# Head 4's second row tile in the opening, and K's block transposes by feature quarters

One core of a Trainium2 chip. The metric is the device time of one execution, in microseconds (us); smaller is better.

## The reference

Sliding-window attention over a cache, between two projections. Eight batches of 32 rows, 32 query heads on 4 K/V heads, a window of the last 2048 keys, 128 features a head, all bf16.

```python
W = min(4096, max(256, Sk // 4))                       # 2048
q = (x @ wq).reshape(B, Sq, Hq, Dh).transpose(0, 2, 1, 3)
k = jnp.repeat(k_cache[:, :, Sk - W:, :], rep, axis=1)
v = jnp.repeat(v_cache[:, :, Sk - W:, :], rep, axis=1)
p = softmax(einsum("bhqd,bhkd->bhqk", q, k) * Dh ** -0.5)
o = einsum("bhqk,bhkd->bhqd", p, v)
return o.transpose(0, 2, 1, 3).reshape(B, Sq, Hq * Dh) @ wo
```

## The kernel before

The 32 pairs of batch and K/V head are "units". A unit has four chunks; a chunk is one step ("slot") of TensorE's program: four matmuls of scores into a PSUM tile `s_ps` (PSUM is the memory that this program's matmuls write to), Exp on ScalarE, and two slots later the product with V. Other work (projections, K's transposes) is put into the slots by a plan. The engines run their instructions in program order.

K must lie with its features on the partitions. Units 0 to 2 get that by TensorE transposes, most others by DMA transposes (`kT`), and the eleven units of `V_T` by VectorE and GpSimd (`kTv`): VectorE turns 32x32 blocks (`blocks`), then 16 moves of 32x512 bring each block row to its partitions (`move`). The numbers of a unit in `V_T`: after which unit's load its raw K is loaded, the slots of the four block transposes, the slots between which the moves lie, and how many moves GpSimd makes.

```python
V_T = {4: (None, (4, 6, 6, 7), 8, 13, 8),
       7: (4, (18, 18, 19, 20), 20, 27, 12), ...
       **{u: (u - 4, range(4*u - 14, 4*u - 10), 4*u - 11, 4*u - 2, 12) for u in (12, 14, ...)}}
...
        def blocks(i):                      # a quarter of the 16 key columns j
            sl = slice(i * KT // 4, (i + 1) * KT // 4)
            nc.vector.transpose(out=st["kb"][:, sl, :], in_=self.k_raw[ui][:, sl, :])
        def move(k, d):                     # needs all four
            out = self.kT[ui][d * 32:(d + 1) * 32, :, k * 32:(k + 1) * 32]
            in_ = st["kb"][k * 32:(k + 1) * 32, :, d * 32:(d + 1) * 32]
            i, n = 4 * k + d, 16 - V_T[ui][4]
            if i * n // 16 != (i + 1) * n // 16:
                nc.vector.tensor_copy(out=out, in_=in_)
            else:
                nc.gpsimd.tensor_scalar(out=out, in0=in_, ...)
...
        # the opening, after x has been transposed
        for c in range(self.DC):            # 8 chunks of wq: all heads, first row tile (heads 0-3: both)
            for h in range(self.rep):
                q_mm(c, h)
        tp = [self.ps_s.tile([P, KT, P], BF16, name="kf_ps", tag="s_ps") for _ in range(2)]
        k_turn(0)                           # eight transposes of K of unit 0
        q_copy(...); q_copy(...); q_copy(...); q_copy(...)
        k_copy(0)                           # VectorE: PSUM to kT, 128x1024
        self.late = self.q_late(4, 2)
        self.late[0]()                      # head 4, second row tile: eight matmuls
        k_turn(1)
        k_copy(1)
...
        # then the slots; slot 0: scores, head 5's second row tile; slot 1: scores, head 6's
```

The pool `ps_s`, of which the score tiles come, has two buffers, and the tiles `tp` of the opening come out of it too.

Of the kernel before, what the change touches and what calls it, by code (L numbers as in the profile page):

```python
# [21 lines left out]

PE_T = (0, 1, 2)

V_T = {4: (None, (4, 6, 6, 7), 8, 13, 8),
       7: (4, (18, 18, 19, 20), 20, 27, 12),
       9: (5, (23, 24, 25, 26), 26, 34, 10),
       **{u: (u - 4, range(4 * u - 14, 4 * u - 10), 4 * u - 11, 4 * u - 2, 12) for u in (12, 14, 17, 19, 22, 24, 27, 29)}}
# [80 lines left out]
class Fast:  # L109
# [72 lines left out]
    def load_k(self, ui, part=None):  # L182
# [3 lines left out]
        src = self.k_cache[b, g, self.Sk - self.W:, :]  # L186
        if ui not in V_T and ui not in self.kT:
            self.kT[ui] = self.ktp.tile([P, KT, P], BF16, name="kT")
        if ui in PE_T or ui in V_T:
            H = KT // 2  # L190
# [58 lines left out]
    def kv_pieces(self, ui):  # L249


        nc, P, KT = self.nc, self.P, self.KT
        st = {}

        def blocks(i):
            if i == 0:
                st["kb"] = self.kbp.tile([P, KT, P], BF16, name="kb")
            sl = slice(i * KT // 4, (i + 1) * KT // 4)
            nc.vector.transpose(out=st["kb"][:, sl, :], in_=self.k_raw[ui][:, sl, :])  # L259

        def move(k, d):
            if k == d == 0:
                self.kT[ui] = self.kvt.tile([P, KT, P], BF16, name="kTv", tag="kv")
            out = self.kT[ui][d * 32:(d + 1) * 32, :, k * 32:(k + 1) * 32]
            in_ = st["kb"][k * 32:(k + 1) * 32, :, d * 32:(d + 1) * 32]
            i, n = 4 * k + d, 16 - V_T[ui][4]
            if i * n // 16 != (i + 1) * n // 16:
                nc.vector.tensor_copy(out=out, in_=in_)  # L268
            else:
                nc.gpsimd.tensor_scalar(out=out, in0=in_, scalar1=1.0, scalar2=1.0, op0=ALU.mult, op1=ALU.mult)  # L270
        return [lambda i=i: blocks(i) for i in range(4)], [lambda k=k, d=d: move(k, d) for k in range(4) for d in range(4)]

    def q_view(self, g):
        return self.QT[g][:, :].rearrange("p (b h s) -> p b h s", b=self.B, h=self.rep)
# [15 lines left out]
        n = 2 if g == 3 else 4  # L290
        return [lambda h=h, i=i: piece(h, i) for h0 in range(0, self.rep, n) for i in range(2) for h in range(h0, h0 + n)]

    def q_late(self, h0, n):
        nc, P, DC, B = self.nc, self.P, self.DC, self.B
        st = {}

        def piece(i):
            if i == 0:
                st["ps"] = self.ps_m.tile([P, n, P], FP32, name="ql_ps", tag="m")
            for c in range(DC):  # L300
                nc.tensor.matmul(st["ps"][:, i, :], lhsT=self.wq_t[0, c // (DC // 2)][:, c % (DC // 2), (h0 + i) * P:(h0 + i + 1) * P],  # L301
                                 rhs=self.xT[:, c, P:self.NQ], start=(c == 0 and i == 0), stop=(c == DC - 1), skip_group_check=True)
            if i == n - 1:
                copy = nc.scalar.copy if h0 == self.rep - 1 else nc.vector.tensor_copy
                copy(out=self.q_view(0)[:, B // 2:, h0:h0 + n, :].rearrange("p b h s -> p h b s"),
                     in_=st["ps"][:, :, :].rearrange("p h (b s) -> p h b s", b=B // 2))
        return [lambda i=i: piece(i) for i in range(n)]

    def o_pieces(self, g, t, cuts=(512, 512), st=None):

# [28 lines left out]
    def start(self):  # L339
        nc, P = self.nc, self.P  # L340
        warm = self.ps_s.tile([P, 512], FP32, name="warm_ps", tag="s_ps")
        one = nc.const_aps.tensor
        x_sb = self.vp.tile([P, self.NT, self.D], BF16, name="x_sb", tag="v")
        xf = self.x.rearrange("b s d -> (b s) d")
        H = self.DC // 2

        nc.sync.dma_start(out=x_sb[:, 0, :], in_=xf[0:P, :])
        nc.scalar.dma_start(out=x_sb[:, 1, :], in_=xf[P:2 * P, :])
        wq0 = self.load_wq(0, 0, (1, 1, 1, 1)) + self.load_wq(0, 1, (2, 1, 1))
        for p in wq0:  # L350
            p()
        self.load_k(0, 0)
        self.load_k(0, 1)
        self.load_v(0, nc.sync)
        self.load_k(1)
        self.weights = []
        for g in range(self.Hkv):
            if g + 1 < self.Hkv:
                self.weights += self.load_wq(g + 1, 0) + self.load_wq(g + 1, 1)
            if g:  # L360
                self.weights += self.load_wo(2 * g - 2) + self.load_wo(2 * g - 1)
        self.weights += self.load_wo(2 * self.Hkv - 2) + self.load_wo(2 * self.Hkv - 1)
        self.load_v(1, nc.sync)
        self.load_k(2)
        self.load_k(4)
        self.load_v(2, nc.sync)
        self.load_unit(3)
        for v in self.va:
            nc.gpsimd.memset(v[:, :, self.Dh:self.VW], 1.0)
        nc.gpsimd.memset(self.ones_c[:, :], 1.0)  # L370
        def warm_up(n):
            for i in range(n):
                nc.tensor.matmul(warm[:, :], lhsT=one(1.0, [P, P], BF16), rhs=one(1.0, [P, 512], BF16), start=True, stop=True)
        warm_up(N_WARM)


        def x_turn(half, pl, tag):
            ps = pl.tile([P, H, self.NT, P], BF16, name="xT_ps", tag=tag)
            for c in range(H):
                for t in range(self.NT):  # L380
                    nc.tensor.transpose(ps[:, c, t, :], x_sb[:, t, half * H + c:self.D:self.DC], self.ident[:, :])  # L381
            for i, copy in ((0, nc.vector.tensor_copy), (1, nc.scalar.copy)):
                c0 = half * H + i * H // 2
                copy(out=self.xT[:, c0:c0 + H // 2, :], in_=ps[:, i * H // 2:(i + 1) * H // 2, :, :].rearrange("p c t s -> p c (t s)"))

        x_turn(0, self.ps_m, "m")
        x_turn(1, self.ps_s, "s_ps")
        qs = [self.ps_o.tile([P, 2, self.NQ], FP32, name="q0_ps", tag="o_ps") for _ in range(2)]
        qs.append(self.ps_m.tile([P, 4, P], FP32, name="q0_ps", tag="m"))
        KT = self.KT  # L390
        tp = None

        def k_turn(half):
            for j in range(half * KT // 2, (half + 1) * KT // 2):
                nc.tensor.transpose(tp[half][:, j % (KT // 2), :], self.k_raw[0][:, j, :], self.ident[:, :])  # L395

        def k_copy(half):
            sl = slice(half * KT // 2, (half + 1) * KT // 2)
            nc.vector.tensor_copy(out=self.kT[0][:, sl, :], in_=tp[half][:, 0:KT // 2, :])

        def q_mm(c, h):
            ps, n = (qs[h // 2][:, h % 2, :], self.NQ) if h < 4 else (qs[2][:, h - 4, :], P)
            nc.tensor.matmul(ps, lhsT=self.wq_t[0, c // H][:, c % H, h * P:(h + 1) * P],  # L403
                             rhs=self.xT[:, c, 0:n], start=(c == 0 and h in (0, 2, 4)), stop=(c == self.DC - 1),
                             skip_group_check=True)

        def q_copy(copy, h0, h1, b0, b1):
            ps = qs[h0 // 2] if h0 < 4 else qs[2]
            copy(out=self.q_view(0)[:, b0:b1, h0:h1, :].rearrange("p b h s -> p h b s"),
                 in_=ps[:, :, b0 * self.Sq:b1 * self.Sq].rearrange("p h (b s) -> p h b s", s=self.Sq))  # L410

        for c in range(self.DC):
            for h in range(self.rep):
                q_mm(c, h)
            if c == 0:
                warm_sb = self.c1.tile([P, 8], BF16, name="warm_sb")
                nc.vector.tensor_copy(out=warm_sb[:, :], in_=warm[:, 0:8])
        tp = [self.ps_s.tile([P, KT, P], BF16, name="kf_ps", tag="s_ps") for _ in range(2)]
        k_turn(0)
        q_copy(nc.scalar.copy, 0, 2, 0, 1)  # L420
        q_copy(nc.vector.tensor_copy, 2, 4, 0, 1)
        q_copy(nc.scalar.copy, 4, 8, 0, 1)
        q_copy(nc.scalar.copy, 4, 8, 1, self.B // 2)
        k_copy(0)
        self.late = self.q_late(4, 2)
        self.late[0]()
        k_turn(1)
        k_copy(1)
        self.va_copy(0)
        q_copy(nc.vector.tensor_copy, 0, 2, 1, self.B)  # L430
        self.q0_rest = lambda: q_copy(nc.vector.tensor_copy, 2, 4, 1, self.B)
# [22 lines left out]
    def side_plan(self):  # L454
# [4 lines left out]
        def spread(pieces, s0, s1):  # L459
            for k, p in enumerate(pieces):  # L460
                plan[s0 + (s1 - s0) * k // len(pieces)].append(p)
# [4 lines left out]
        for g, w in Q_SLOTS.items():  # L466
            pieces = self.q_pieces(g)
            n = 0 if g == 3 else 4
            spread(pieces[:n], *w[0])
            spread(pieces[n:], *w[1])  # L470
        for g, w in O_SLOTS.items():
            spread(self.o_pieces(g, 0) + (self.o_pieces(g, 1) if g < self.Hkv - 1 else []), *w)
        for ui, (_, s0, s1, s2, _) in V_T.items():
            blocks, moves = self.kv_pieces(ui)
            for k, p in enumerate(blocks):
                plan[s0[k]].append(p)
            spread(moves, s1, s2)
        return plan

    def run(self):  # L480
# [214 lines left out]
```

## Time and profile before

| | before |
|---|---|
| median of the first three executions | 183.78 us (183.70 to 184.23) |
| span of the profiled execution | 182.3 us |
| TensorE / VectorE / ScalarE / GpSimd busy | 97% / 69% / 75% / 49% |
| GpSimd's wait for VectorE's block transposes | 32.1 us in 8 places |

TensorE is the bound. The other engines' idle time is of no account unless TensorE waits for them.

### The profile page before, as it was taken

Reading aid. Unit: us, or ns where it says so; the run is one execution under the profiler, and the core shown is the slowest. Engines: PE = TensorE matmul, PEld = TensorE weight load, DVE = VectorE, ACT = ScalarE, POOL = GpSimd, SP = SyncE. Lnnn points to the kernel's source line nnn. Section 1 sums busy time; section 2 is a strip of 40 time slices with the busy share of each in tenths; the row PEclk is TensorE's granted clock in tenths of the full one; section 3 lists DMA queues with packets and bytes.
Section 4 is the critical chain, followed back from the end, with each engine's and each line's share of the span. In section 5 each row is a group of like instructions: output and inputs, shape, how many; then the busy total and the mean of one; then the engine's idle time right before and its main releaser. Section 6 shows DMA issues by size and latency. Waiting matters only on the chain.

```text
span 182.3 us, 5017 instructions
## 1 busy us (share of the span) xinstructions
PE 177.4 (97%) x2026; PEld 152.0 (83%) x2041; DVE 126.0 (69%) x257; ACT 136.2 (75%) x147; POOL 89.2 (49%) x138
## 2 busy tenths in 40 slices
PE   7999999999999999999999999999999999999993
PEld 2899998998999999988787899988787788888853
DVE  0237799769887698487799565967587987554253
ACT  2228898896897888997878787887878788888800
POOL 2003564088770895936939707929606949600000
PEclk9999999999999999999999999999999999999999
DMA  6999999999999999999999999999999999980013
GB/s 169 395 400 408 225 388 350 233 296 260 377 391 244 322 257 365 374 295 313 304 378 377 391 269 271 369 245 365 258 318 273 331 289 344 218 167 0 0 41 85
DMA packets 52954, 51.73 MB, mean 284 GB/s; under 512 B 39744, under 2 KB 40256, under 8 KB 52928
## 3 DMA queue, kind: packets, MB, share of 16 engines
q1 hardware_dynamic: 52352, 50.90, 99.3%
q10 hardware_dynamic: 576, 0.49, 0.8%
q8 instruction: 16, 0.26, 0.6%
q14 instruction: 10, 0.08, 0.1%
HBM read 41.42 MB, written 0.52 MB: 230 GB/s over the span
## 4 chain that ended last, share of the span: by engine, by line
PE 91%; DMA 6%; SPq 1%; issue 1%; DVE 0%
PE o_ps L516 30%; PE s_ps L505 30%; PE op_ps L322 14%; PE q_ps L285 10%; DMA kT<-in_k_cache_dram 4%; PE q_ps L403 3%; DMA x_sb<-in_x_dram 2%; PE ql_ps L301 1%; PE tp L244 1%; SPq L208 1%; PE xT_ps L381 1%; PE kf_ps L395 0%; SPq L200 0%; DVE o_t L332 0%; PE cnt_ps L571 0%
## 5 line engine op out<-in xcount | busy, mean ns | idle before, releaser
L507 ACT ACTIVATE pT<-s_ps 128x1024 bf16<-128x1024 f32 x128 | 128.3, 1027 | 27.7 <-PE s_ps L505 27.4
L270 POOL TENSOR_SCALAR kTv<-kb 32x512 bf16<-32x512 bf16 x126 | 84.3, 669 | 51.3 <-DVE kb L259 32.1
L516 PE MATMUL o_ps<-va,pT 128*128 128x129 bf16 x1024 | 78.8, 220 | 0.1
L516 PEld LDWEIGHTS <-pT 128*128 128x128 bf16 x1024 | 68.5, 98 | 3.1
L505 PE MATMUL s_ps<-QT,kT 128*128 128x256 bf16 x336 | 50.4, 273 | 0.2
L505 PEld LDWEIGHTS <-kT 128*128 128x128 bf16 x336 | 31.7, 98 | 9.8 <-DMA kT<-in_k_cache_dram 0.4
L322 PE MATMUL op_ps<-wo_sb,OT 128*128 128x512 bf16 (+2 forms) x129 | 32.8, 353 | 0.6
L259 DVE STREAM_TRANSPOSE kb<-k_raw 128x512 bf16<-128x512 bf16 x44 | 29.7, 691 | 1.6 <-DMA k_raw<-in_k_cache_dram 1.2
L285 PE MATMUL q_ps<-xT,wq_sb 128*128 128x256 bf16 x192 | 28.3, 273 | 0.0
L438 DVE COPY va<-v_sb 128x2048 bf16<-128x2048 bf16 x30 | 25.4, 847 | 2.0 <-DMA v_sb<-in_v_cache_dram 1.6
L505 PE MATMUL s_ps<-QT,kTv 128*128 128x256 bf16 x176 | 26.4, 273 | 0.2
L268 DVE COPY kTv<-kb 32x512 bf16<-32x512 bf16 x50 | 23.1, 462 | 1.2
L444 DVE RECIPROCAL RL_all<-o_ps 128x2 f32<-128x2 f32 x32 | 5.3, 165 | 26.3 <-PE o_ps L516 26.1
L505 PEld LDWEIGHTS <-kTv 128*128 128x128 bf16 x176 | 16.9, 98 | 6.5 <-issue 0.4
L285 PEld LDWEIGHTS <-wq_sb 128*128 128x128 bf16 x192 | 16.9, 98 | 1.2
L450 DVE STREAM_TRANSPOSE OT<-o_sb 128x256 bf16<-128x256 bf16 x32 | 14.3, 445 | 1.1
L448 DVE TENSOR_TENSOR o_sb<-o_ps,RL_all 128x256 bf16<-128x256 f32 x32 | 13.6, 424 | 1.1
L322 PEld LDWEIGHTS <-OT 128*128 128x128 bf16 x144 | 11.4, 98 | 2.3 <-DVE OT L450 0.2
L436 POOL TENSOR_SCALAR va<-v_sb 128x2048 bf16<-128x2048 bf16 x2 | 3.8, 1897 | 17.0 <-DMA v_sb<-in_v_cache_dram 17.0
L288 ACT CAST QT<-q_ps 128x512 bf16<-128x512 f32 x12 | 7.0, 583 | 0.2 <-PE q_ps L285 0.2
L329 DVE TENSOR_TENSOR oacc<-op_ps,oacc 128x512 f32<-128x512 f32 x8 | 5.3, 662 | 2.0 <-PE op_ps L322 2.0
L332 DVE TENSOR_TENSOR o_t<-op_ps,oacc 128x512 bf16<-128x512 f32 (+2 forms) x6 | 3.1, 514 | 3.8 <-remote 2.2
(35 smaller groups left out, 45.0 us busy)
## 6 DMA issues: line engine op xcount, KB each, us to landing
v_sb<-in_v_cache_dram SPq DMA_DIRECT2D x30, 512.0 KB, 6.6
wo_sb<-in_wo_dram SPq DMA_DIRECT2D x16, 512.0 KB, 6.4
wq_sb<-in_wq_dram SPq DMA_DIRECT2D x13, 512.0 KB, 6.6
k_raw<-in_k_cache_dram SPq DMA_DIRECT2D x13, 512.0 KB, 5.7
wq_sb<-in_wq_dram SPq DMA_DIRECT2D x6, 256.0 KB, 4.5
v_sb<-in_v_cache_dram SPq DMA_DIRECT2D x4, 256.0 KB, 5.2
kT<-in_k_cache_dram SPq DMA_TRANSPOSE x36, 7.1
k_raw<-in_k_cache_dram SPq DMA_DIRECT2D x2, 256.0 KB, 5.7
```

The costliest lines, as they stand in the source:

```text
L259: nc.vector.transpose(out=st["kb"][:, sl, :], in_=self.k_raw[ui][:, sl, :])
L268: nc.vector.tensor_copy(out=out, in_=in_)
L270: nc.gpsimd.tensor_scalar(out=out, in0=in_, scalar1=1.0, scalar2=1.0, op0=ALU.mult, op1=ALU.mult)
L285: nc.tensor.matmul(st[k][:, hl % 2, :], lhsT=self.wq_t[g, i][:, c % (DC // 2), hl * P:(hl + 1) * P], rhs=self.xT[:, c, :], start=(c == 0 a ...
L288: nc.scalar.copy(out=self.q_view(g)[:, :, 2 * k:2 * k + 2, :].rearrange("p b h s -> p h b s"), in_=st[k][:, :, :].rearrange("p h (b s) -> ...
L322: nc.tensor.matmul(ps[:, 0:w], lhsT=self.OT[:, gq, c, t * P:(t + 1) * P], rhs=self.wo_t[gq][:, c, n0:n0 + w], start=(k == 0), stop=(k == 7))
L438: self.nc.vector.tensor_copy(out=out, in_=in_)
L448: nc.vector.tensor_tensor(out=o_sb[:, :, :, :], in0=o_ps[:, :, 0:Dh].rearrange("p q (i c) -> p q c i", c=4), in1=rl[:, ui * QT_N:(ui + 1) ...
L450: nc.vector.transpose(out=self.OT[:, g * QT_N:(g + 1) * QT_N, :, b * self.Sq:(b + 1) * self.Sq], in_=o_sb[:, :, :, :])
L505: nc.tensor.matmul(s_ps[:, jj, :], lhsT=self.kT[ui][:, c * CJ + jj, :], rhs=q_u, start=True, stop=True)
L507: nc.scalar.activation(out=pT[:, :, :], in_=s_ps[:, :, :], func=ACT.Exp, bias=0.0, scale=self.scale)
L516: nc.tensor.matmul(o_ps[:, qt, 0:self.VW], lhsT=pT[:, jj, qt * P:(qt + 1) * P], rhs=va[:, j, 0:self.VW], start=(j == 0 and qt == 0), stop= ...
```

## The change

x has 256 rows, two row tiles of 128. The intent of the change: (1) to do head 4's second row tile in the projection loop, where TensorE waits for wq, and to copy K out in quarters, so that the first scores start sooner; (2) to let GpSimd move K when one feature quarter has been turned, and not all four, and to give VectorE the moves of the last quarter alone.

```diff
-V_T = {4: (None, (4, 6, 6, 7), 8, 13, 8),
+V_T = {4: (None, (4, 6, 6, 7), 8, 13, 9),
@@ blocks and moves
-            sl = slice(i * KT // 4, (i + 1) * KT // 4)
-            nc.vector.transpose(out=st["kb"][:, sl, :], in_=self.k_raw[ui][:, sl, :])
+            sl = slice(i * P // 4, (i + 1) * P // 4)
+            nc.vector.transpose(out=st["kb"][:, :, sl], in_=self.k_raw[ui][:, :, sl])
-            i, n = 4 * k + d, 16 - V_T[ui][4]
-            if i * n // 16 != (i + 1) * n // 16:
+            if 4 * d + k >= V_T[ui][4]:
-        return ..., [... for k in range(4) for d in range(4)]
+        return ..., [... for d in range(4) for k in range(4)]
@@ opening (q_late takes the chunks to do as an argument)
+        self.late = self.q_late(4, 2)
         for c in range(self.DC):
             for h in range(self.rep):
                 q_mm(c, h)
+            self.late[0](cs=(c,))
...
-        k_copy(0)
-        self.late = self.q_late(4, 2)
-        self.late[0]()
+        k_copy(nc.vector.tensor_copy, 0, KT // 4)
+        k_copy(nc.vector.tensor_copy, KT // 4, KT // 2)
         k_turn(1)
-        k_copy(1)
+        k_copy(nc.vector.tensor_copy, KT // 2, KT)
@@ side_plan
-            spread(moves, s1, s2)
+            spread(moves[:n], s0[1] + 1, s2)
+            spread(moves[n:], s1, s2)
```

More of the change, by code (lines that the diff above doesn't have):

```diff
@@ L270, in move @@
                 nc.gpsimd.tensor_scalar(out=out, in0=in_, scalar1=1.0, scalar2=1.0, op0=ALU.mult, op1=ALU.mult)
-        return [lambda i=i: blocks(i) for i in range(4)], [lambda k=k, d=d: move(k, d) for k in range(4) for d in range(4)]
+        return [lambda i=i: blocks(i) for i in range(4)], [lambda k=k, d=d: move(k, d) for d in range(4) for k in range(4)]
     def q_view(self, g):
@@ L291, in q_pieces, with q_late, piece @@
         return [lambda h=h, i=i: piece(h, i) for h0 in range(0, self.rep, n) for i in range(2) for h in range(h0, h0 + n)]
-    def q_late(self, h0, n):
+    def q_late(self, h0, n, st=None):
         nc, P, DC, B = self.nc, self.P, self.DC, self.B
-        st = {}
-        def piece(i):
-            if i == 0:
+        st = {} if st is None else st
+        def piece(i, cs=None):
+            if "ps" not in st:
                 st["ps"] = self.ps_m.tile([P, n, P], FP32, name="ql_ps", tag="m")
-            for c in range(DC):
+            for c in range(DC) if cs is None else cs:
                 nc.tensor.matmul(st["ps"][:, i, :], lhsT=self.wq_t[0, c // (DC // 2)][:, c % (DC // 2), (h0 + i) * P:(h0 + i + 1) * P],
@@ L306, in piece @@
                      in_=st["ps"][:, :, :].rearrange("p h (b s) -> p h b s", b=B // 2))
-        return [lambda i=i: piece(i) for i in range(n)]
+        return [lambda i=i, **kw: piece(i, **kw) for i in range(n)]
     def o_pieces(self, g, t, cuts=(512, 512), st=None):
@@ L395, in k_turn, with k_copy @@
                 nc.tensor.transpose(tp[half][:, j % (KT // 2), :], self.k_raw[0][:, j, :], self.ident[:, :])
-        def k_copy(half):
-            sl = slice(half * KT // 2, (half + 1) * KT // 2)
-            nc.vector.tensor_copy(out=self.kT[0][:, sl, :], in_=tp[half][:, 0:KT // 2, :])
+        def k_copy(copy, j0, j1):
+            copy(out=self.kT[0][:, j0:j1, :], in_=tp[2 * j0 // KT][:, j0 % (KT // 2):j0 % (KT // 2) + j1 - j0, :])
         def q_mm(c, h):
@@ L472, in side_plan @@
             spread(self.o_pieces(g, 0) + (self.o_pieces(g, 1) if g < self.Hkv - 1 else []), *w)
-        for ui, (_, s0, s1, s2, _) in V_T.items():
+        for ui, (_, s0, s1, s2, n) in V_T.items():
             blocks, moves = self.kv_pieces(ui)
```

## The prediction

> **What bounds the kernel now.** I read the page first: row 1 (engines), row 2 (slices) and row 4 (the chain that ended last).
>
> ```profile
> span 182.3 us, 5017 instructions
> PE 177.4 (97%) x2026; PEld 152.0 (83%) x2041; DVE 126.0 (69%) x257; ACT 136.2 (75%) x147; POOL 89.2 (49%) x138
> DMA  6999999999999999999999999999999999980013
> PE 91%; DMA 6%; SPq 1%; issue 1%; DVE 0%
> ```
>
> TensorE is 91% of the chain and neither VectorE (69% busy) nor GpSimd (49%) is near its limit. So work that moves between VectorE and GpSimd is worth only what a TensorE wait on it costs. What can be won is TensorE's idle time, and I looked for all of it by going through the timeline from 4.4 us (first transposes of x) to the end, comparing the distance between two matmul starts with what the same pair takes elsewhere (0.056 us behind a 128-column matmul, 0.11 us behind a 256-column one). I found four places of over 0.05 us behind the opening's x transposes that the change could touch, 0.16 + 0.06 + 0.27 + 0.29 = 0.78 us in all, 0.4% of the span:
>
> ```profile
> 8.64 0.61 PEld L403 LDWEIGHTS <-wq_sb 128*128 128x128 bf16 x7 [0.16 <-DMA wq_sb<-in_wq_dram]
> ...
> 12.69 0.33 PEld L505 LDWEIGHTS <-kT 128*128 128x128 bf16 x4
> ...
> 26.94 3.25 DVE L268 COPY kTv<-kb 32x512 bf16<-32x512 bf16 x6
> ...
> 30.31 0.34 PEld L505 LDWEIGHTS <-kTv 128*128 128x128 bf16 x4 [0.36 <-issue]
> ```
>
> First line: in the opening's Q projection TensorE stands 0.16 us for the second half of wq. Second: the first scores start at 12.69, 0.06 us later than the dense row of transposes before them would allow; the copy of K out of PSUM (11.94 + 0.69 = 12.63) holds them. Third and fourth: the scores of unit 4 start when VectorE's last move of that unit's transposed K is done, 26.94 + 3.25 = 30.19; the dense row would have put the matmul at 30.07, and it started at 30.34, so 0.27 us are lost. GpSimd's moves were done at 29.75.
>
> The fourth wait decides this prediction. It comes from the chain of waits, in order of time, window 43 to 44.2 us:
>
> ```profile
> 36.74 6.67 DMA kT<-in_k_cache_dram
> 43.42 0.05 issue
> 43.46 0.61 PE s_ps L505 x4
> ```
>
> Chunk 2 of unit 6 waits for the second half of its K, which the DMA transpose lands at 43.42; TensorE would have been ready at about 43.17, 0.29 us sooner. Is that transfer late because a buffer came free late, or because the DMA engines are full? The table by stretches (columns after the five engines: TensorE clock, DMA share, GB/s):
>
> ```profile
> 2.50:10.00 7.50, 7.33 (x70) 5.26 (x69) 0.92 (x3) 1.07 (x2) 0.00 (x0) 1.00 1.02 383
> 10.00:20.00 10.00, 10.00 (x147) 9.53 (x145) 5.95 (x12) 6.87 (x10) 1.90 (x1) 1.00 1.11 354
> 20.00:30.00 10.00, 10.00 (x140) 9.47 (x137) 9.71 (x19) 9.23 (x11) 7.16 (x9) 1.00 1.05 365
> 30.00:40.00 10.00, 9.89 (x122) 9.05 (x120) 8.07 (x19) 8.32 (x11) 2.77 (x5) 1.00 1.17 261
> ```
>
> The share is over 1.0 in all of them: the 16 DMA engines are full from 2.5 us on, so the queue runs as fast as it can and the landing at 43.42 does not depend on how soon TensorE comes. Walking the program's load order, no transfer ahead of this one reuses a buffer that is freed later than it is needed: unit 6's kT takes unit 0's, v of unit 6 that of unit 0.
>
> **What the skill says.** The Trainium skill, "SBUF — State Buffer", section "Who interferes with whom": a VectorE copy in a two-port mode and a GpSimd instruction exclude each other for a whole instruction, and DMA contends with neither. The trace agrees on the first: VectorE's 32x512 moves take 0.283 us at the least and up to 0.661 beside GpSimd's (median 0.582, window 18 to 47), and one GpSimd move was drawn out from 0.61 to 0.95 us by a copy of V. "VectorE: DVE Perf Modes", section "The three transpose paths": VectorE's transpose turns 32x32 blocks only. That is why the 16 moves per unit exist, and why a transposed feature quarter is all that four of the moves need. "Perfetto Trace Analysis", section "Optimization Strategy": find the gaps on the bounding engine and what releases them; that is the method above.
>
> **The change, part by part.** *Opening, matmuls.* Eight 128-column matmuls of head 4's second row tile move from between the two K transposes into the projection loop, one per chunk. In the loop they cost 8 x 0.056 = 0.45 us. Four of them come before the wq wait, 4 x 0.056 = 0.22, and cover its 0.16. The loop so ends 0.45 - 0.16 = 0.29 us later, and the K transposes start at 11.24 + 0.29 = 11.53 in place of 11.24. But these eight were what TensorE did while VectorE copied K. After the change only the second eight transposes (0.45 us) lie there. *Opening, copies.* The copy of 128x1024 in 0.69 us becomes two of 128x512; the x copy of that shape (PSUM to SBUF, bf16) takes 0.424 each, and two of those back to back overlap by about 0.08 (13.44 + 0.68 against a next start at 14.04), so 0.34 + 0.42 = 0.77. The copy began 0.70 us after the transposes began (11.94 - 11.24); so now 12.23, first quarter done at 12.65, second at 12.99. The first score tile takes the PSUM buffer of this very tile (two buffers, taken in turn), so I expect it to wait for both: 12.99 + 0.05 = 13.04 in place of 12.69, 0.35 later. The eight matmuls are done before 12.69 in both kernels, so none of that is made up: TensorE simply stands about 0.6 us there. If only the first quarter counts, the start is 12.70 and nothing is lost or won.
>
> *Unit 4.* GpSimd gets 9 moves for 8, VectorE 7 for 8, and GpSimd's begin behind block quarter 0 (19.23 + 0.71 = 19.94) and not behind the fourth (23.21 + 0.69 = 23.90). Two of its moves come in program order before its copy of V for unit 2: 2 x 0.67 = 1.34, so that copy starts near 21.3 and not 20.60, ends near 23.3, and the first matmul that reads it is at 24.15: no wait. The other 7 moves end at 23.3 + 7 x 0.67 + 0.34 (one drawn out) = 28.3. VectorE keeps its order with one move fewer; its five behind 26.94 run beside GpSimd until 28.3 and then at 0.28: done about 28.9, over 1 us ahead of need. The 0.27 wait goes.
>
> *Units 7 to 29.* 12 or 10 moves per unit start up to 5 us sooner on GpSimd (its 32.1 us of waiting on VectorE's blocks mostly end), but TensorE had no wait for these units: nothing on the path. Block transposes of 128 x (16 runs of 32) keep 512 elements a lane; I estimate 0.67 to 0.75 us as now (0.691).
>
> *Sum.* TensorE reaches unit 6, chunk 2 at 43.17 + 0.35 - 0.27 = 43.25, or with the kinder opening at 42.9. Both are before 43.42. It waits there and starts at 43.46 as before, and everything behind it is the same dense row of matmuls. Net change: 0. A gain of 0.2 to 0.5 us in the first 30 us is given back in a wait for DMA.
>
> **The rivals.** (1) *The gains add up to the end*: 0.27, with the kinder opening perhaps 0.3 to 0.4, and the time is 183.4. For it: the DMA landing varies between executions, and where it comes sooner, gains pass. Against it: shares over 1.0 for 40 us, and unit 5's second half lands at 37.65 for a need at 37.86, so a second transfer stands close behind the first. (2) *VectorE or GpSimd becomes late somewhere*: more contention while V is copied (0.65 us alone, 1.04 beside GpSimd), or strided transposes cost much more than 0.69; at 0.1 us each, 44 of them add 4.4 us to VectorE's 126, which 56 idle us take up; a stall of a unit or two would add 0.3 to 1 us: 184.3. (3) *The opening costs more than 0.6 us net*, so that TensorE is behind the DMA at 43.4: plus 0.1 to 0.3 us. Against it: the path above is short.
>
> **Range and chances.** The three times of before lie at 183.70, 183.78 and 184.23, so half a microsecond is noise. Centre 183.7: no change from 183.78, with a small part of rival 1. Low 183.2 is rival 1 in full with some noise, high 184.3 is rival 2 or the slow one of the three. 2% is 3.7 us, nearly five times all the idle time that I found, and no new wait of that size is in sight: within 2% 0.98, 0.01 on either side.
>
> **What would show it.** In the changed trace: no wait on wq at 8.6; K transposes near 11.5; first scores near 13.0 (right) or 12.7 (buffer rule wrong); GpSimd's first move near 20 and unit 4's scores without a gap; the wait for kT of unit 6 grown to between 0.2 and 0.6 us, with its start still near 43.4; the same distances from there to the end. The prediction is wrong if that start moves with TensorE, or if a wait on kTv, va or o_ps turns up behind 44 us.

## The result

| | before | changed |
|---|---|---|
| median | 183.74 us (183.55 to 184.23, 4 runs) | 183.94 us (183.76 to 184.15, 4 runs) |
| span of the profiled execution | 182.3 us | 182.1 us |
| ratio | | 1.0007, 95% interval 0.9984 to 1.0030 |

A ratio is the mean time of one kernel's fast runs over that of the other's of the same rounds, so not quite the ratio of the medians. The changed kernel takes the same time within noise. Its page:

```profile
span 182.1 us, 5033 instructions
PE 178.0 (98%) x2041; PEld 152.1 (84%) x2041; DVE 125.3 (69%) x257; ACT 136.3 (75%) x147; POOL 89.8 (49%) x139
DMA  5999999999999999999999999999989999990003
PE 93%; DMA 3%; SPq 1%; DVE 1%; issue 0%
```

DMA fell from 6% to 3% of the chain and VectorE came in with 1%. Both have a place in the timeline. First the projection loop (timeline of the changed kernel, 4.2 to 9.4 us):

```profile
8.83 0.66 PEld L401 LDWEIGHTS <-wq_sb 128*128 128x128 bf16 x8 [0.28 <-DMA wq_sb<-in_wq_dram]
```

The wait for wq is still there. Four of the moved matmuls lie ahead of it, but wq landed at 8.79 in this execution and at 8.60 in the other. Then the first scores (timeline, 11 to 15.1 us):

```profile
11.66 0.94 PEld L394 LDWEIGHTS <-k_raw 128*128 128x128 bf16 x16
...
12.36 1.35 DVE L397 COPY kT<-kf_ps 128x512 bf16<-128x512 bf16 x3 [0.50 <-PE kf_ps L394]
...
13.17 0.33 PEld L505 LDWEIGHTS <-kT 128*128 128x128 bf16 x4 [0.57 <-DVE kT L397]
```

All sixteen transposes now come in one row and TensorE then idles 0.57 us for VectorE's copies: this is the chain's new 1%. The first scores start at 13.17 and not 12.69. The first quarter's copy ended at 12.78 (12.36 + 0.425), the second's at 13.12; the scores followed the second. Unit 4, with VectorE's moves and the loads of its scores (timeline, 26.9 to 31.7 us):

```profile
27.05 2.24 DVE L267 COPY kTv<-kb 32x512 bf16<-32x512 bf16 x5
...
30.45 0.42 PEld L505 LDWEIGHTS <-kTv 128*128 128x128 bf16 x4
```

Its K is complete at 29.29, and the scores' load no longer shows a wait. GpSimd's timeline between 19 and 30 us tells why:

```profile
20.11 1.30 POOL L269 TENSOR_SCALAR kTv<-kb 32x512 bf16<-32x512 bf16 x2 [1.43 <-DVE RL_all L443]
21.49 1.90 POOL L435 TENSOR_SCALAR va<-v_sb 128x2048 bf16<-128x2048 bf16 x1
23.48 5.07 POOL L269 TENSOR_SCALAR kTv<-kb 32x512 bf16<-32x512 bf16 x7
```

Two moves run behind the first block quarter, ahead of the copy of V; the other seven are done at 28.55, where before eight ran from 24.05 to 29.75. Unit 6, chunk 2, in the chain of waits between 43 and 44.2 us:

```profile
42.98 0.17 PE o_ps L516 x3
43.16 0.44 PE q_ps L284 x4
43.59 0.44 PE s_ps L505 x4
```

No DMA any more: these scores start at 43.43 (the chain prints 43.59, where the matmul ahead of them has ended), in their turn in the dense row. The transfer landed at 41.86.

GpSimd's waits for the block transposes, before and changed (`--waits`: us in total, times, longest), and the block transposes themselves, before and changed (page, with the mean ns of one):

```profile
POOL kTv L270 <- DVE kb L259: 32.1, 8, 7.3
POOL kTv L269 <- DVE kb L259: 27.2, 7, 7.1
L259 DVE STREAM_TRANSPOSE kb<-k_raw 128x512 bf16<-128x512 bf16 x44 | 29.7, 691 | 1.6 <-DMA k_raw<-in_k_cache_dram 1.2
L259 DVE STREAM_TRANSPOSE kb<-k_raw 128x512 bf16<-128x512 bf16 x44 | 29.5, 687 | 1.0 <-DMA k_raw<-in_k_cache_dram 0.7
```

Most of the waiting that the change went for is still there. GpSimd has as much to do as before (49% busy) and now idles mostly ahead of a unit's first quarter, not ahead of its fourth. What grew is the margin: from the last move of a unit's K to the unit's first scores it is 0.20 to 1.76 us for the units 9 to 29 of `V_T` in this trace of before, and 2.73 to 5.13 us in that of the changed kernel.

### The profile page after: what moved, and what is told of

Read it like the earlier page. It is cut to its first block, busy times and chain, and to the rows that moved or that the text cites. A ratio compares the mean times of both kernels' runs of the same rounds, so it can differ in the third digit from the quotient of the medians.

```text
span 182.1 us, 5033 instructions
## 1 busy us (share of the span) xinstructions
PE 178.0 (98%) x2041; PEld 152.1 (84%) x2041; DVE 125.3 (69%) x257; ACT 136.3 (75%) x147; POOL 89.8 (49%) x139
## 4 chain that ended last, share of the span: by engine, by line
PE 93%; DMA 3%; SPq 1%; DVE 1%; issue 0%
PE o_ps L516 32%; PE s_ps L505 31%; PE op_ps L321 15%; PE q_ps L284 12%; DMA wq_sb<-in_wq_dram 3%; PE q_ps L401 2%; PE tp L244 1%; SPq L168 1%; PE ql_ps L300 1%; DVE kT L397 0%; PE kf_ps L394 0%; SPq L346 0%; DVE o_t L331 0%; PE cnt_ps L571 0%
## 5 line engine op out<-in xcount | busy, mean ns | idle before, releaser
L507 ACT ACTIVATE pT<-s_ps 128x1024 bf16<-128x1024 f32 x128 | 128.4, 1028 | 27.2 <-PE s_ps L505 26.9
L269 POOL TENSOR_SCALAR kTv<-kb 32x512 bf16<-32x512 bf16 x127 | 84.9, 669 | 47.7 <-DVE kb L259 27.2
L321 PE MATMUL op_ps<-wo_sb,OT 128*128 128x512 bf16 (+2 forms) x144 | 36.0, 355 | 0.0
L284 PE MATMUL q_ps<-xT,wq_sb 128*128 128x256 bf16 x192 | 28.3, 273 | 0.0
L267 DVE COPY kTv<-kb 32x512 bf16<-32x512 bf16 x49 | 22.6, 462 | 1.2
L435 POOL TENSOR_SCALAR va<-v_sb 128x2048 bf16<-128x2048 bf16 x2 | 3.8, 1900 | 15.2 <-DMA v_sb<-in_v_cache_dram 15.1
L401 PE MATMUL q_ps<-xT,wq_sb 128*128 128x256 bf16 (+1 forms) x64 | 5.9, 246 | 0.1
```

The source lines that it names most:

```text
L269: nc.gpsimd.tensor_scalar(out=out, in0=in_, scalar1=1.0, scalar2=1.0, op0=ALU.mult, op1=ALU.mult)
L284: nc.tensor.matmul(st[k][:, hl % 2, :], lhsT=self.wq_t[g, i][:, c % (DC // 2), hl * P:(hl + 1) * P], rhs=self.xT[:, c, :], start=(c == 0 a ...
L321: nc.tensor.matmul(ps[:, 0:w], lhsT=self.OT[:, gq, c, t * P:(t + 1) * P], rhs=self.wo_t[gq][:, c, n0:n0 + w], start=(k == 0), stop=(k == 7))
L401: nc.tensor.matmul(ps, lhsT=self.wq_t[0, c // H][:, c % H, h * P:(h + 1) * P], rhs=self.xT[:, c, 0:n], start=(c == 0 and h in (0, 2, 4)), ...
L507: nc.scalar.activation(out=pT[:, :, :], in_=s_ps[:, :, :], func=ACT.Exp, bias=0.0, scale=self.scale)
```

## The experiments

Most effects here are a few tenths of a microsecond, and the time of one kernel scatters by half a microsecond or more between executions. So I measured distances inside the traces. "Chunk 4" is the first matmul of the projection's chunk 4, behind the wait for wq; behind it no distance depends on when wq landed. "Scores 0", "scores 4" and "scores 31" are the first matmuls of scores of these units. "Waits on kTv" are TensorE waits on VectorE's and GpSimd's moves.

| trace | chunk 4 at | to scores 0 | on to scores 4 | on to scores 31 | chunk 4 to scores 31 | waits on kTv |
|---|---|---|---|---|---|---|
| before, first | 8.64 | 4.04 | 17.65 | 137.44 | 159.14 | unit 4: 0.27 |
| before_again | 8.89 | 4.05 | 17.38 | 137.46 | 158.89 | unit 17: 0.32 |
| changed | 8.84 | 4.33 | 17.38 | 137.18 | 158.90 | none |
| e1_opening | 9.30 | 4.32 | 17.38 | 137.14 | 158.85 | none |
| e2_quarters | 8.62 | 4.11 | 17.39 | 137.20 | 158.69 | none |
| e3_onekf | 8.93 | 4.77 | 17.43 | 137.14 | 159.34 | none |
| f4_filled | 8.69 | 4.33 | 17.33 | 137.28 | 158.94 | none |
| f5_between | 9.21 | 4.11 | 17.38 | 137.14 | 158.64 | none |
| f6_onecopy | 8.87 | 4.26 | 17.38 | 137.14 | 158.78 | none |
| f7_nostart | 9.05 | 4.33 | 17.38 | 137.14 | 158.85 | none |
| g1_before_plus8 | 8.79 | 4.48 | 17.38 | 137.56 | 159.42 | unit 7: 0.41 |
| g2_after_plus8 | 8.75 | 4.77 | 17.38 | 137.39 | 159.54 | none |
| g3_best | 9.18 | 3.76 | 17.43 | 137.14 | 158.33 | none |

17.38 and 137.14 are the dense rows: many traces have just these, so anything above is a wait. The distances end at unit 31. From its scores to the end of the span it is 14.33 to 14.35 us in eight traces, 14.43 in g1 and g2, 14.50 in the first trace of before, 14.65 in e3_onekf and 14.72 in f7_nostart; what makes these five longer was not looked into. Timed runs:

| run | median, us | before, same rounds | ratio | 95% interval |
|---|---|---|---|---|
| e1_opening | 184.40 | 184.14 | 1.0033 | 0.9995 to 1.0071 |
| e2_quarters | 183.87 | 184.14 | 0.9994 | 0.9964 to 1.0023 |
| e3_onekf | 184.93 | 184.14 | 1.0064 | 1.0034 to 1.0094 |
| g1_before_plus8 | 184.74 | 184.09 | 1.0037 | 1.0012 to 1.0063 |
| g2_after_plus8 | 184.52 | 184.09 | 1.0029 | 1.0005 to 1.0053 |
| g3_best | 183.92 | 184.09 | 0.9985 | 0.9967 to 1.0003 |

The changed kernel itself was not timed again in these rounds, so it is compared with the others by its trace alone. before_again and f4 to f7 had one look each (184.62; 184.53, 184.54, 183.78, 184.40), whose state is unknown, and whose times say nothing at this size. All outputs were correct.

**The opening alone.** `V_T`, blocks, moves and plan of before in the changed kernel:

```diff
-V_T = {4: (None, (4, 6, 6, 7), 8, 13, 9),
+V_T = {4: (None, (4, 6, 6, 7), 8, 13, 8),
-            sl = slice(i * P // 4, (i + 1) * P // 4)           # and the rest of kv_pieces
+            sl = slice(i * KT // 4, (i + 1) * KT // 4)
-            spread(moves[:n], s0[1] + 1, s2)
-            spread(moves[n:], s1, s2)
+            spread(moves, s1, s2)
```

> The change's opening with the block transposes and moves of before. Theory A (the opening costs 0.35 to 0.48 us and the unit 4 part wins 0.27 only where TensorE comes early): first scores near 13.15, TensorE so late that unit 4's K (ready near 30.2) no longer holds it, unit 4's scores near 30.55 without a gap, unit 6 chunk 2 near 43.4, time that of the changed kernel, within 0.15 us. Theory B (the two parts simply add): 0.27 us slower than the changed kernel.

Unit 4's scores had no gap, and chunk 4 to scores 31 took 158.85, as in the changed kernel: theory A. The clock times of the expectation failed (13.63 for 13.15): in this execution TensorE ran x's transposes at 0.107 us each and not 0.061 (so it did in f7_nostart and g3_best) and was half a microsecond late from the start. That is why the distances count. That the times agree within 0.15 us was not tested.

**The block quarters alone.** The change's moves, and the opening of before:

```diff
-        k_copy(nc.vector.tensor_copy, 0, KT // 4)              # and the rest of the opening
-        k_copy(nc.vector.tensor_copy, KT // 4, KT // 2)
+        k_copy(0)
+        self.late = self.q_late(4, 2)
+        self.late[0]()
```

> The opening of before with the change's block transposes and moves. Theory A: first scores near 12.69, unit 4's scores at 30.07 without a gap; from there only a late K transfer (unit 5 or 6) can hold TensorE. If these transfers land as in the trace of before (43.42), unit 6 chunk 2 starts at 43.46 and the time is that of before; if as in the changed kernel's trace (41.86), it starts near 42.9 and the time is 0.3 to 0.5 us under the changed kernel's. Theory B (the unit 4 part is worth nothing or costs something): not faster than the kernel before, and a gap before unit 4's scores stays.

The second branch came: first scores at 12.72, unit 4 at 30.11 without a gap, the transfer for unit 6 landed at 41.31, its scores started at 42.94. Its size did not: from chunk 4 it is 0.21 us shorter than the changed kernel, where 0.3 to 0.5 was expected. The times (0.9994) are too coarse to confirm it.

**Before**, nothing edited.

> The kernel before, unchanged, for a second trace of it. Theory A (its wait at 43.46 is for a transfer whose landing differs between executions): first scores 12.69 and the gap before unit 4's scores again, 0.27; the K transfer of unit 6 may land anywhere between 41.8 and 43.5, so the gap at unit 6 chunk 2 between 0 and 0.3. Rival (the landing is fixed by a full queue): 43.4 again.

Half of it held. The transfer landed at 41.33 and chunk 2 of unit 6 started at 43.15 with no wait, so 43.42 was that first execution's own. In twelve of the thirteen traces, of all kernels, this transfer landed between 41.31 and 41.90. The gap before unit 4 was gone as well, since wq had come at 8.84 and TensorE was 0.25 us later at scores 0, just enough. A new one stood before unit 17. VectorE's timeline of before_again, 87.6 to 95.5 us:

```profile
89.91 1.09 DVE L438 COPY va<-v_sb 128x2048 bf16<-128x2048 bf16 x1 [1.56 <-DMA v_sb<-in_v_cache_dram]
91.03 0.59 DVE L268 COPY kTv<-kb 32x512 bf16<-32x512 bf16 x1
...
94.55 0.29 DVE L268 COPY kTv<-kb 32x512 bf16<-32x512 bf16 x1
```

VectorE stands 1.56 us for V, everything behind it in program order is late, and the last move for unit 17 ends at 94.84, with the scores at 94.98. In the changed kernel VectorE stands as long for V, 1.79 us, but its last move for unit 17 lies ahead in the program of what piles up behind:

```profile
90.72 0.88 DVE L437 COPY va<-v_sb 128x2048 bf16<-128x2048 bf16 x1 [1.79 <-DMA v_sb<-in_v_cache_dram]
91.63 0.58 DVE L267 COPY kTv<-kb 32x512 bf16<-32x512 bf16 x1
92.24 0.71 DVE L259 STREAM_TRANSPOSE kb<-k_raw 128x512 bf16<-128x512 bf16 x1
```

The move at 91.63 is the last. Unit 17 has 2.73 us in hand (92.21 to 94.94), unit 4 has 1.25 (29.30 to 30.55), unit 7 has 1.47 (44.61 to 46.08); in the first trace of before these were 0.50, none, and 0.65.

**One PSUM tile for K's first transposes**, so that the first score tile has the other buffer:

```diff
-        tp = [self.ps_s.tile([P, KT, P], BF16, name="kf_ps", tag="s_ps") for _ in range(2)]
+        tp = self.ps_s.tile([P, KT, P], BF16, name="kf_ps", tag="s_ps")
-                nc.tensor.transpose(tp[half][:, j % (KT // 2), :], self.k_raw[0][:, j, :], self.ident[:, :])
+                nc.tensor.transpose(tp[:, j, :], self.k_raw[0][:, j, :], self.ident[:, :])
```

> The changed kernel with both halves of K's first transposes in one PSUM buffer, so that the first score tile takes the other buffer. Theory A (the first scores wait for both quarter copies because they reuse that buffer): first scores behind the first quarter copy, 0.33 us sooner than in the changed kernel, near 12.84, second chunk near 13.8; time 0.1 to 0.3 us lower. Rival (the scores need both quarters for another reason, or the wait is for data): first scores stay near 13.17.

Both failed; the kernel is slower, 1.0064. Its timeline, 11.5 to 14.9 us:

```profile
12.45 0.76 DVE L397 COPY kT<-kf_ps 128x512 bf16<-128x512 bf16 x2 [0.50 <-PE kf_ps L394]
...
13.26 0.61 PE L394 MATMUL kf_ps<-ident,k_raw 128*128 128x128 bf16 x8 [0.84 <-DVE kT L397]
```

Now the second eight transposes wait for both copies of the first eight, though they write the other half of the tile. The wait is the program's own: in the records of the kept trace the first of these transposes waits for VectorE's semaphore S[109], and of the two copies only the second raises it; it ends at 13.20, and the transpose starts at 13.26. In the changed kernel the load of the first scores waits for the same semaphore, which there both copies raise. The trace does not show the count it waits for, but the load starts at 13.17, 0.05 us behind the end of the second copy. So this run cannot tell whether it is the reuse of the buffer that ties the scores to the second quarter. That the scores wait for the second quarter's copy, by a semaphore, is shown; that the buffer is why the program asks for it stays argued from the program.

**The hole filled.** Head 5's eight matmuls before the scores, head 6's one slot sooner:

```diff
-Q_LATE = {6: 1, 7: 9}
+Q_LATE = {6: 0, 7: 9}
         k_copy(nc.vector.tensor_copy, KT // 2, KT)
+        self.late[1]()
-        plan[0].append(self.late[1])
```

> The changed kernel with head 5's second row tile (eight matmuls) put into the hole before the first scores, and head 6's one slot sooner. Theory A (the copies of K set the first scores, and ScalarE's first Exp sets the third chunk of scores, 1.78 us behind the first): the hole of 0.57 us before the first scores shrinks to about 0.12, they start no sooner (4.33 us behind the first matmul of chunk 4 of the projection), a hole of about 0.45 us opens before the third chunk instead, and the distance from that matmul to unit 31's scores stays at 158.9. Rival (idle TensorE time in the opening is what costs): 158.45, 0.45 us less.

Theory A: the hole shrank to 0.12, scores 0 stayed at 4.33, chunk 4 to scores 31 at 158.94. The hole came back two chunks on, with ScalarE's name on it (timeline, 12.2 to 15.1 us):

```profile
14.75 0.60 PE L505 MATMUL s_ps<-QT,kT 128*128 128x256 bf16 x4 [0.23 <-ACT pT L507]
```

The third chunk of scores needs the tile that the first Exp reads, and that Exp starts behind scores 0. What counts in the opening is when scores 0 start, and not how full TensorE is before them. (This trace also lost 0.13 us to a transfer for unit 5.)

**The eight matmuls back between the transposes**, quarter copies kept; and **one copy in place of two**, the rest kept:

```diff
-            self.late[0](cs=(c,))
+        self.late[0]()
         k_turn(1)
```

```diff
-        k_copy(nc.vector.tensor_copy, 0, KT // 4)
-        k_copy(nc.vector.tensor_copy, KT // 4, KT // 2)
+        k_copy(nc.vector.tensor_copy, 0, KT // 2)
```

> The changed kernel with the eight matmuls back between the two K transposes; the two quarter copies and the rest of the change stay. Theory A: from the first matmul of chunk 4 to the first scores 4.05 us as in the kernel before plus 0.07 for the second copy, 4.12 in place of 4.33; to unit 31's scores 158.7, as in the run with the quarters alone. Rival (the quarter copies are the cost): 4.33 stays.

> The changed kernel with the first half of K copied out in one copy again. Theory A: the first scores start 4.26 us behind the first matmul of chunk 4 in place of 4.33. Rival (the scores go on behind the first quarter, and it is worth something): later than 4.33.

4.11 and 4.26: both as theory A had it. The opening's loss behind the wait for wq, 4.33 - 4.05 = 0.28 us, is so taken apart: 0.22 for the four matmuls of the second half of the loop (they push K's transposes back, 2.65 to 2.87 behind chunk 4), 0.07 for the second copy. Distances of this size scatter: the same opening took 4.04 and 4.05 us in the traces of before and 4.11 in e2_quarters, where K's transposes start 2.70 behind chunk 4 and not 2.65. The 0.07 rests also on the copies' own times, 0.76 for two and 0.69 for one. The four ahead of the wait cost nothing where wq is late.

**GpSimd's earlier place in the program taken back:**

```diff
-            spread(moves[:n], s0[1] + 1, s2)
+            spread(moves[:n], s1, s2)
```

> The changed kernel, but GpSimd's moves put into the program only where the other moves begin; order by feature quarters and block transposes by quarters stay. Theory A (what matters is that VectorE's last moves come sooner in its order and GpSimd's first moves need one quarter only): unit 4's K is done near 29.3 on VectorE and near 28.9 on GpSimd, no gap before its scores, unit 17's K done 2 us or more ahead of its scores; same distances as the changed kernel. Rival (the earlier place in the program is what removes the wait): a gap before unit 4's or unit 17's scores returns.

Unit 4's K was done at 29.50 on VectorE and 28.75 on GpSimd, unit 17's at 92.04 with the scores at 95.11, no gaps. In this trace the earlier place is not needed; dependence on one quarter and VectorE's order are enough together. Which of these two counts was not separated.

**A delay of eight transposes in both kernels:**

```diff
+        for j in range(8):
+            nc.tensor.transpose(tp[1][:, j, :], self.k_raw[0][:, j, :], self.ident[:, :])
         k_turn(0)
```

> The kernel before with eight idle transposes (0.45 us of TensorE) ahead of K's own. Theory A (before has waits for kT later that take up a delay; both its traces lose 0.27 to 0.3 us to them): first scores 4.49 us behind the first matmul of chunk 4 (4.05 + 0.45), no gap before unit 4's scores, 154.5 from the first scores to unit 31's; from chunk 4 to unit 31's scores 159.0, that is no more than the 158.9 to 159.1 of before: 0.45 us of work for nothing to 0.1. Rival (TensorE is dense, each delay shows in full): 159.35 to 159.6.

> The changed kernel with the same eight transposes ahead of K's own. Theory A (nothing behind the first scores waits any more): first scores 4.78 us behind the first matmul of chunk 4, 154.5 from there to unit 31's scores, so 159.3 from chunk 4, the full 0.45 more than 158.9. Rival (waits take it up here too): 158.9 to 159.0.

The opening went as said (4.48, 4.77), the rest did not. Before with the delay lost unit 4's gap, but found another, this time on GpSimd (its timeline, 44.9 to 47.2 us):

```profile
46.54 0.33 PEld L507 LDWEIGHTS <-kTv 128*128 128x128 bf16 x4 [0.53 <-POOL kTv L270]
```

GpSimd's last move for unit 7 ended at 46.49. (The chain names the Exp of the chunk just ahead, which ended at 46.53. By the program, with two score tiles, scores need the Exp of two chunks before, and elsewhere they start while the last Exp still runs: in the changed kernel at 30.55, with an Exp from 29.93 to 30.95.) So 159.42 and not 159.0: here the waits of the kernel before did not take up the delay, one turned up at another unit. The changed kernel with the delay took 159.54 for 159.3; it lost 0.16 and 0.07 us to two DMA transfers near 90 and 120 us. The pair does not separate the theories as I had put them, and in time they are alike (1.0037, 1.0029).

**Both parts put right:** the change's moves; in the loop only the four matmuls ahead of the wait for wq; K's first transposes inside the last chunk of the loop, so that one copy runs under the rest of it; the other four matmuls between the transposes.

```diff
             for h in range(self.rep):
                 q_mm(c, h)
-            self.late[0](cs=(c,))
+                if c == self.DC - 1 and h == 1:
+                    tp = [...]                                  # as before
+                    k_turn(0)
+            if c < self.DC // 2:
+                self.late[0](cs=(c,))
...
+        k_copy(nc.vector.tensor_copy, 0, KT // 2)               # ahead of q_copy
...
+        self.late[0](cs=range(self.DC // 2, self.DC))
         k_turn(1)
```

> The change's block transposes and moves; in the opening only the four of head 4's eight matmuls that lie ahead of the wait for wq stay in the loop, K's first transposes go into the last chunk of the loop, so that the copy of K (one copy) runs under the rest of the loop, and the other four matmuls lie between the two K transposes. Theory A: first scores 3.77 to 3.85 us behind the first matmul of chunk 4 (4.33 in the changed kernel, 4.05 before), 158.3 from there to unit 31's scores (158.9), so some 0.5 us faster than both where wq lands alike. Rival (VectorE's two copies or ScalarE's hold the first scores as long as before): 4.05 or more.

Chunk 4 to scores 0 took 3.76 and to scores 31 158.33 us, 0.57 less than in the changed kernel. Its timeline, 11 to 14.6 us:

```profile
12.03 0.69 DVE L397 COPY kT<-kf_ps 128x1024 bf16<-128x1024 bf16 x1 [5.14 <-PE kf_ps L394]
...
12.90 0.35 PEld L507 LDWEIGHTS <-kT 128*128 128x128 bf16 x4
```

The copy ends at 12.72 and no wait is left before the scores. Its span, 181.8, is 0.2 us above that of e2_quarters, but chunk 4 started 0.56 later. Its chain is 98% TensorE, with no DMA. In time it is 0.9985 of before, interval 0.9967 to 1.0003: whether it is faster is not clear.

## Why the prediction was right

The number and the range held (183.94 for 183.7, range 183.2 to 184.3). That the gain ends in nothing held too, but not in the place that the prediction named, and by its own test ("The prediction is wrong if that start moves with TensorE") its main mechanism failed. That a loss of 0.28 in the opening met a gain of about the same size is luck. By its steps:

- *K's transposes pushed back by 0.45 less the covered wait.* Behind chunk 4 it is exactly the four matmuls, 0.22. That the wait for wq would go was wrong in this trace (0.28 left), because wq landed 0.19 later and TensorE had begun the loop 0.15 sooner (5.70 for 5.85): 0.16 - 0.22 + 0.19 + 0.15 = 0.28. f6_onecopy shows no such wait. Wq landed between 8.46 and 9.16 and the loop began between 5.59 and 6.15 in the thirteen traces, so this wait is chance.
- *First scores at 13.04 behind both quarter copies, a hole of about 0.6.* Measured 13.17 and 0.57. The size of the copies (0.76 together) was right; the eight matmuls had been what hid them.
- *Unit 4's gap of 0.27 goes; its K done near 28.9.* The gap went; the K was done at 29.30, 0.4 later than said, and still 1.25 ahead of need. GpSimd's first move at 20.11 (20), the copy of V ending at 23.39 (23.3), its last move at 28.54 (28.3).
- *Block transposes as dear as now.* 687 ns for 691.
- *GpSimd's 32.1 us of waiting mostly end.* Wrong: 27.2 us stayed. It cost nothing, as the prediction said of all idle time off the path.
- *The step that failed: TensorE waits at unit 6, chunk 2 for a landing at 43.42 in any case.* It started there at 43.43, which looks like a hit, and is not: the transfer had landed at 41.86, and TensorE came at that time by itself, at 43.17 + 0.48 - 0.27, with some 0.05 of small differences. The start did move with TensorE: it was 42.94, 43.15, 43.43 and 43.96 in e2_quarters, before_again, the changed kernel and e3_onekf, with first scores at 12.72, 12.94, 13.17 and 13.70. The moment of a landing from one trace was taken for a fixed one. Nothing is "given back in a wait for DMA"; the gain was spent in the opening, 0.28 behind the wait for wq.
- *A step that was missing: units 7 to 29 have nothing on the path.* True of the one trace that I had. Three of the four traces with the old moves have one wait on kTv of 0.27 to 0.41 us, each at another unit (4, 17, 7); none of the nine with the new moves has one. So the second part does more than close unit 4's gap: it takes away waits that come and go with the margins of several units. In e1_opening, with the old moves and the later opening, there was none to take away.

The failed step rested on two readings that the prediction's own trace does not bear. The first is that the DMA engines are full because their share is over 1.0. In shorter stretches of the same trace the share is 2.30 in one, which cannot be a busy share, and 0.50 in another, where 166 GB/s were moved (383 in the prediction's first row):

```profile
36.00:38.00 2.00, 2.00 (x27) 1.85 (x25) 1.18 (x4) 2.00 (x3) 0.95 (x2) 1.00 0.50 166
42.00:43.40 1.40, 1.33 (x17) 0.99 (x14) 1.35 (x3) 1.10 (x2) 1.27 (x3) 1.00 2.30 283
```

The second is that the queue does not wait for TensorE. The issues of K's DMA transposes (L200) do, 17.0 us in 9 places over the whole execution (`--waits --engine SP`):

```profile
SPq L200 <- PE s_ps L505: 17.0, 9, 4.6
```

Two of these waits, 1.2 us in all, lie between 24 and 43 us, and one of them ends at 34.50, in the chain just ahead of this transfer. The landing itself did not follow TensorE all the same: in the other twelve traces, with first scores from 12.72 to 13.70, it came at 41.31 to 41.90 (41.86 for 13.17, 41.57 for 13.70). Why it came at 43.42 in the one is open.

The account of the change behind chunk 4 is then: opening +0.28; waits on kTv -0.27 (first trace) or -0.32 (second); and, against the first trace alone, a DMA wait of 0.29 that was chance. That makes 158.86 and 158.85, where 158.90 was measured (159.14 and 158.89 before). Rival 1, that gains pass to the end, was the right mechanism for unit 4; there was only a loss of the same size beside it.

What stays open: whether the buffer or something else ties the first scores to the second quarter, why one landing came 1.5 us behind the other twelve, and, in timed runs, any of the differences below 0.3%; only the traces show those.

## What to carry to other kernels

Work put into a wait of the bounding engine may have been hiding something where it was: ask what ran beside it, and move only the part that lies ahead of the wait. In an engine that runs in order, what counts for a consumer is where the last piece stands in the program, behind which other waits; here a margin of half a microsecond in one trace (unit 17) was a wait in the next. Take a second trace of the same kernel before building on the time of one transfer.

## What the Trainium skill lacked or had wrong

- "DMA: Bandwidth & Descriptors" gives rates and latencies, but no spread between executions. Here the same transfer, in the same place of the queue and issued between 35.32 and 37.25 us, landed at 41.31 to 41.90 us in twelve traces and at 43.42 in one (issued at 36.74); wq landed between 8.46 and 9.16.
- "VectorE: DVE Perf Modes", section "The three transpose paths", does not say what strided blocks cost. Here nothing: 687 ns for 16 runs of 32 elements a partition, 691 for 512 in a row.
